# Loading the convolution's tap weights on ScalarE's DMA queue and converting them first, in a fused attention and gated FFN kernel

## Chip, cores and metric

One core of one Trainium2 chip. The metric is the device time of one execution in microseconds (us), median over runs; lower is better.

## What is computed

Inputs are float32 in kind, but the weights `w_in`, `conv_w` and `w_out` come as 64-bit floats, viewed as pairs of 32-bit words.

```python
# 4 batches, 8 heads, 768 positions, head width 64; chunks of 32 queries
for c in range(nc):                       # a window of 16 + 32 + 8 keys and 8 memory keys
    scores = scale * q_c @ k_full.T
    a = softmax(scores)
    out[:, :, c_start:c_end] = a @ v_full
x = out as (batch, 768, 512)
h = np.maximum(x @ w_in, 0.0)             # 512 -> 1024
conv_out = sum(conv_w[k] * hp[:, k:k + S] for k in range(3))   # 3 taps for each of 1024 channels
gate = 1.0 / (1.0 + np.exp(-conv_out))
return h * gate @ w_out                   # 1024 -> 512
```

## The kernel before

The work is cut into 32 attention pieces (batch, half of the sequence, pair of heads), 32 blocks of hidden channels (batch, 128 channels), and the output products. Matmul operands are kept as two parts, high and low, so that three matmuls make one product. `from_f64` makes the two parts from the two 32-bit words of each weight: it loads a tile `w` (pool `w64`, 4 buffers), makes a working copy `w_top` (2 buffers) with an absolute value on ScalarE (L306), and then goes through integer and float steps on VectorE, GpSimd and ScalarE. It is called once for the tap weights (128x24, kind `s`), 8 times for `w_in` and 8 times for `w_out` (128x512 each). The last step for the taps adds the two parts into `cw` (L815), from which the gating of every block of channels takes its three taps (L598 and L602 for the middle one, L607 for the outer ones).

Each engine runs its instructions in the order in which they are written, and that order is fixed by hand: the functions first register 1818 operations in a list (`plan.op`), numbered as they are registered, and `Plan.run` then issues them in the sequence of the table `ORDER`. Operations 0 to 10 are the tap weights: 0 the load, 1 the absolute value, 2 a maximum on GpSimd (L310), 3 to 6 four steps on VectorE (L316, L323, L342, L371), 7 an add on GpSimd (L377), 8 the high part on ScalarE (L379), 9 the low part on GpSimd (L382), 10 the sum `cw` on VectorE (L815). Operations 570 on are `w_in`. All loads of the kernel are issued by SyncE (SP), in the order of the same table. Buffers of a pool are handed out first in, first out, when an operation first needs one.

Ahead of the plan ScalarE makes `minus`, a negated identity (L283), with the load of its function table before it, and GpSimd clears some buffers.

The first operations of `ORDER` before are

```python
ORDER = [
    570, 571, 572, 573, 580, 574, 581, 582, 0, 583, 586, 12, 575, 11, 577, 587, 584, 588, 29, 585, 28, 45, 14, 15,
```

with operations 1 to 10 spread over the following lines.

Of the kernel before, what the change touches and what calls it, by code (L numbers as in the profile page):

```python
# [11 lines left out]
U32 = mybir.dt.uint32  # L12
# [199 lines left out]
RATE = 405  # L212
# [11 lines left out]
def attention_then_gated_ffn(  # L224
# [10 lines left out]
    nc = tc.nc  # L235
# [14 lines left out]
    plan = Plan()  # L250
# [36 lines left out]
    def load(dst, src, w):  # L287
        size = 1
        for x in src.shape:
            size *= x  # L290
        plan.op("DMA", size * 4 / RATE, lambda: nc.sync.dma_start(out=dst(), in_=src), w=w)

    def from_f64(src, hi, lo, key, n, kind):
        w = Tile("w64")
# [646 lines left out]
```

## Time and profile before

| | |
|---|---|
| time, median of 3 runs | 337.82 us (336.71 to 338.04) |
| the profiled execution's own time | 337.24 us |
| its span, first to last instruction | 335.5 us |
| TensorE busy (PE) | 322.1 us, 96% of the span |
| VectorE busy (DVE) | 296.4 us, 88% |
| ScalarE busy (ACT) | 222.6 us, 66% |
| GpSimd busy (POOL) | 51.2 us, 15% |
| granted TensorE clock | 0.998 of full |
| moved by DMA | 60.87 MB, all of the kernel's own on one queue, q1 |

PE counts matmuls, PEld the loads of their stationary operand, SPq the DMA issues of SyncE. A time on the timeline is counted from the start of the span. The execution's own time is 1.7 us longer than its span.

### The profile page before, as it was taken

The page shows a single profiled execution, that of the slowest core. Times are in us where ns is not written, and L with a number is a line of the kernel's source. Part 1 is how long each engine was busy: PE and PEld are TensorE (multiplying, and loading weights), DVE is VectorE, ACT ScalarE, POOL GpSimd, SP SyncE. Part 2 cuts the span into 40 slices and gives each one's busy share as a digit, 9 for nine tenths or more (in the row PEclk, how much of TensorE's full clock was granted, in tenths as well). Part 3 has the DMA queues.
Part 4 walks back from the last instruction along what each step waited for, and adds up shares of the span by engine and source line. Part 5 has one row for each costly group of instructions (what it writes and reads, how often), then busy time and mean ns, then how long its engine had stood idle before and what let it go on. Part 6 is the DMA issues. An engine that isn't in the chain of part 4 may idle for free.

```text
span 335.5 us, 8308 instructions
## 1 busy us (share of the span) xinstructions
PE 322.1 (96%) x3259; PEld 305.1 (91%) x3259; DVE 296.4 (88%) x516; ACT 222.6 (66%) x502; POOL 51.2 (15%) x72
## 2 busy tenths in 40 slices
PE   0899999999999999999999999999999999999995
PEld 0689999999999999899988878999999999999995
DVE  3998998999999989899999999999999999599311
ACT  3588896887787879759787527658886486355210
POOL 2150310302104010410020312000000600700000
PEclk9999999999999999999999999999999999999999
DMA  8999998699697969650412545131032642011013
GB/s 278 401 372 345 388 342 291 218 300 293 202 328 230 295 193 342 218 167 34 129 61 80 195 134 198 75 146 47 2 109 64 195 135 96 26 56 63 33 65 110
DMA packets 31144, 60.87 MB, mean 181 GB/s; under 512 B 3584, under 2 KB 18048, under 8 KB 31104
## 3 DMA queue, kind: packets, MB, share of 16 engines
q1 hardware_dynamic: 31104, 60.33, 53.3%
q8 instruction: 26, 0.43, 0.5%
q14 instruction: 14, 0.11, 0.1%
HBM read 47.93 MB, written 12.39 MB: 180 GB/s over the span
## 4 chain that ended last, share of the span: by engine, by line
PE 89%; DMA 5%; DVE 2%; ACT 2%; issue 1%; SPq 0%; ACTq 0%
PE f L577 38%; PE f L736 15%; PE f L793 10%; PE s L736 7%; PE ta L540 7%; PE s L427 6%; PE ta L736 4%; DMA w<-in_w_out_dram 2%; PE ta L491 2%; DMA out_dram<-k 1%; DMA w<-in_w_in_dram 1%; ACT e L462 1%; ACT w_top L306 0%; PE f L355 0%; DVE w_top L323 0%
## 5 line engine op out<-in xcount | busy, mean ns | idle before, releaser
L577 PE MATMUL f<-u,w_in_hi 128*128 128x384 f32 x512 | 140.8, 343 | 0.6 <-ACT u L587 0.6
L577 PEld LDWEIGHTS f<-u,w_in_hi 128*128 128x128 f32 x512 | 93.2, 188 | 2.7 <-ACT u L587 1.1
L577 PE MATMUL f<-u,w_in_lo 128*128 128x384 f32 x256 | 86.0, 336 | 0.0
L607 DVE SCALAR_TENSOR_TENSOR u<-u,cw,u 128x767 f32<-128x767 f32 x64 | 64.4, 1027 | 0.1
L577 PEld LDWEIGHTS f<-u,w_in_lo 128*128 128x128 f32 x256 | 48.2, 188 | 0.2
L644 DVE TENSOR_TENSOR u<-u,u 128x768 fp32r<-128x768 f32 (+1 forms) x55 | 46.5, 871 | 0.8 <-ACT u L641 0.8
L641 ACT CAST u<-u 128x768 fp32r<-128x768 f32 (+1 forms) x56 | 41.1, 765 | 8.3 <-PE s L736 2.8
L736 PE MATMUL f<-w_in_hi,u 128*128 128x256 f32 x216 | 45.0, 282 | 0.0
L587 ACT ACTIVATE u<-f 128x384 f32<-128x384 f32 x64 | 30.6, 490 | 15.9 <-PE f L577 15.0
L736 PEld LDWEIGHTS f<-w_in_hi,u 128*128 128x128 f32 x216 | 36.0, 188 | 0.0
L616 DVE SCALAR_TENSOR_TENSOR u<-u,u 128x768 f32<-128x768 f32 x32 | 31.4, 993 | 0.4 <-ACT u L611 0.4
L793 PE MATMUL f<-w_out_hi,u 128*128 128x512 f32 x96 | 31.6, 397 | 0.0
L462 ACT ACTIVATE e<-s,top 128x64 f32<-128x64 f32 x132 | 29.3, 324 | 3.4 <-DVE w L509 1.6
L611 ACT ACTIVATE u<-u 128x768 f32<-128x768 f32 x32 | 26.8, 847 | 6.1 <-DVE u L607 6.0
L736 PE MATMUL f<-w_in_lo,u 128*128 128x256 f32 x108 | 30.3, 281 | 0.0
L598 ACT ACTIVATE u<-u,cw 128x768 f32<-128x768 f32 x30 | 28.3, 944 | 2.7 <-DVE z L476 1.3
L479 POOL TENSOR_TENSOR e<-e,z 128x384 f32<-128x384 f32 x22 | 20.6, 936 | 54.1 <-DVE z L476 35.3
L753 ACT COPY w<-f 128x256 f32<-128x256 f32 x18 | 6.6, 374 | 27.3 <-PE f L736 22.8
L427 PE MATMUL s<-k,u 128*64 128x64 f32 x672 | 24.7, 224 | 0.0
L427 PEld LDWEIGHTS s<-k,u 128*64 128x64 f32 x672 | 21.8, 138 | 3.1 <-issue 2.2
L759 DVE TENSOR_TENSOR k<-s,w 128x256 f32<-128x256 f32 x18 | 7.6, 422 | 17.1 <-PE s L736 9.6
L651 POOL TENSOR_TENSOR u<-u,u 128x384 f32<-128x384 f32 x9 | 10.8, 1200 | 74.6 <-DVE u L616 62.0
(99 smaller groups left out, 609.6 us busy)
## 6 DMA issues: line engine op xcount, KB each, us to landing
u<-in_q_dram SPq DMA_DIRECT2D x32, 384.0 KB, 6.2
u<-in_v_dram SPq DMA_DIRECT2D x25, 384.0 KB, 5.4
k<-in_k_dram SPq DMA_DIRECT2D x28, 252.0 KB, 4.9
out_dram<-k SPq DMA_DIRECT2D x36, 128.0 KB, 1.7
w<-in_w_in_dram SPq DMA_DIRECT2D x8, 512.0 KB, 6.7
w<-in_w_out_dram SPq DMA_DIRECT2D x8, 512.0 KB, 5.9
y_dram<-u SPq DMA_DIRECT2D x8, 384.0 KB, 2.8
u<-y_dram SPq DMA_DIRECT2D x8, 384.0 KB, 3.4
```

What stands on the lines that cost most here:

```text
L427: nc.tensor.matmul(s.t[j * D : (j + 1) * D, o : o + KW], lhsT=q_[:, c], rhs=k_t.t[:, c * STEP : c * STEP + KW], start=True, stop=True,)
L462: A.activation(keys(e)[:, g // 2, g % 2], s_()[:, g // 2, g % 2], AF.Exp, bias=top.t[:, g : g + 1], scale=SCALE)
L577: nc.tensor.matmul(f.t[:, :TW], lhsT=w_in_p[c][:, part, col : col + P], rhs=x.t[:, a * TW : (a + 1) * TW], start=(cc == 0 and i == 0), sto ...
L587: "A", act(TW, True), lambda: A.activation(h.t[:, hf * TW : (hf + 1) * TW], f.t[:, :TW], AF.Relu, scale=0.5), (f,), ((h, hf),)
L598: plan.op("A", act(S, ptr=1), lambda: A.activation(c.t, h.t, AF.Copy, scale=w[1]), H, (c,))
L607: lambda j=j, to=to, at=at: V.scalar_tensor_tensor(out=c.t[:, to], in0=h.t[:, at], scalar=w[j], in1=c.t[:, to], op0=ALU.mult, op1=ALU.add) ...
L611: plan.op("A", act(S), lambda: A.activation(c.t, c.t, AF.Tanh), (c,), (c,), table="exp")
L616: lambda: V.scalar_tensor_tensor(out=y.t, in0=c.t, scalar=1.0, in1=h.t, op0=ALU.add, op1=ALU.mult),
L641: plan.op("A", act(n), lambda: A.copy(out=hi(), in_=src()), (y,), (k_hi,))
L644: lambda: (V if eng == "V" else G).tensor_tensor(out=low(), in0=src(), in1=hi().bitcast(F32), op=ALU.subtract),
L736: nc.tensor.matmul(ps.t[:, :n], lhsT=l[a](), rhs=w[c], start=(first and j == 0 and m == 0), stop=(j == hf - 1 and m == 2), skip_group_chec ...
L793: nc.tensor.matmul(ps.t[:, :n], lhsT=gs[b, fc][a].t[:, tt * P : (tt + 1) * P], rhs=w_out_p[c][:, fc, o : o + n], start=(fc == 0 and i == 0 ...
```

## The change

The tap weights' load is issued from ScalarE's queue and not from SyncE's, and operations 0 to 10 stand first in `ORDER`. All other operations keep their order among themselves.

```diff
 ORDER = [
-    570, 571, 572, 573, 580, 574, 581, 582, 0, 583, 586, 12, 575, 11, 577, 587, 584, 588, 29, 585, 28, 45, 14, 15,
+    0, 1, 2, 3, 4, 5, 6, 7, 8, 9, 10, 570, 571, 572, 573, 580, 574, 581, 582, 583, 586, 12, 575, 11, 577, 587, 584,
...
-    def load(dst, src, w):
+    def load(dst, src, w, queue=nc.sync):
         size = 1
         for x in src.shape:
             size *= x
-        plan.op("DMA", size * 4 / RATE, lambda: nc.sync.dma_start(out=dst(), in_=src), w=w)
+        plan.op("DMA", size * 4 / RATE, lambda: queue.dma_start(out=dst(), in_=src), w=w)
...
-        load(lambda: w.t[:, :n].rearrange("p n w -> p (n w)"), src.bitcast(U32), (w,))
+        load(lambda: w.t[:, :n].rearrange("p n w -> p (n w)"), src.bitcast(U32), (w,), nc.scalar if key == "cw2" else nc.sync)
```

On ScalarE, at the start of the program, the difference reads as follows (`w_89` to `w_92` are the four buffers of pool `w64`, `w_top_93` and `w_top_94` the two of the working copy, `cw_hi` the taps' high part; lines with - stood there before, lines with + now).

```order
 L283 ACT_TABLE_LOAD
 L283 ACTIVATE w_out_hi<-ident 128x128
-L306 ACTIVATE w_top_93<-w_89 128x512
+L291 DMA w_89<-in_conv_w_dram 128x48
+L306 ACTIVATE w_top_93<-w_89 128x24
+L379 CAST cw_hi<-w_top_93 128x24
 L306 ACTIVATE w_top_94<-w_90 128x512
```

The load's issue, the taps' absolute value and their high part have moved in front of the first absolute value of `w_in`, and behind the table load and `minus`.

VectorE began before with the first block of `w_in`:

```order
L936 UNCONDITIONAL_BRANCH
L310 TENSOR_SCALAR w_top_93<-w_top_93 128x512
L316 TENSOR_SCALAR w_top_93<-w_top_93 128x512
L323 SCALAR_TENSOR_TENSOR w_top_93<-w_89,w_top_93 128x512
L310 TENSOR_SCALAR w_top_94<-w_top_94 128x512
```

and begins now with the taps:

```order
L936 UNCONDITIONAL_BRANCH
L316 TENSOR_SCALAR w_top_93<-w_top_93 128x24
L323 SCALAR_TENSOR_TENSOR w_top_93<-w_89,w_top_93 128x24
L342 TENSOR_SCALAR w_89<-w_top_93 128x24
L371 SCALAR_TENSOR_TENSOR w_89<-w_89 128x24
L815 TENSOR_TENSOR cw<-cw_hi,cw_lo 128x24
L310 TENSOR_SCALAR w_top_94<-w_top_94 128x512
L316 TENSOR_SCALAR w_top_94<-w_top_94 128x512
```

All five of the taps' steps on VectorE now stand ahead of the 11 steps of `w_in` and of the first maximum over scores (L436), which followed those 11 before and follows them now.

## Rows read from the trace of the kernel before

**Rows 1.** Chain of waits, first 26 us: start us, us, what.
```profile
4.43 0.67 ACT w_top L306
...
5.12 0.44 DVE w_top L310
...
5.58 0.44 DVE w_top L316
...
10.60 0.48 DVE top L436
...
13.82 1.55 PE s L427 x24
...
19.30 0.85 PE s L427 x24
```
**Rows 2.** All waits of TensorE: waited for, us in total, times, longest us.
```profile
PE s L427 <- DMA u<-in_q_dram: 7.7, 1, 7.7
PE s L427 <- DVE e L441: 0.9, 1, 0.9
PE f L577 <- ACT u L587: 0.6, 1, 0.6
PE s L427 <- ACT e L462: 0.6, 1, 0.6
```
**Rows 3.** ScalarE's timeline from the start: start us, us, instruction, [idle before].
```profile
0.72 1.28 ACT L283 ACT_TABLE_LOAD   x1 [0.72 <-PEq L928]
2.02 0.31 ACT L283 ACTIVATE w_out_hi<-ident 128x128 fp32r<-128x128 f32 x1
```
**Rows 4.** SyncE's timeline: the issue of the tap weights' load.
```profile
1.64 0.42 SPq L291 DMA_DIRECT2D w<-in_conv_w_dram  x1
```
**Rows 5.** DMA issues of the whole run: count, KB each, median us to landing.
```profile
out_dram<-k SPq DMA_DIRECT2D x36, 128.0 KB, 1.7
...
w<-in_conv_w_dram SPq DMA_DIRECT2D x1, 24.0 KB, 4.2
```
**Rows 6.** DMA issues in the first microsecond.
```profile
w<-in_w_in_dram SPq DMA_DIRECT2D x1, 512.0 KB, 3.7
```
**Rows 7.** Busy time by stretch; the last two columns are DMA share and GB/s.
```profile
2.70:4.40 1.70, 0.00 (x0) 0.00 (x0) 0.00 (x0) 0.00 (x0) 0.16 (x6) 1.00 0.97 378
```
**Rows 8.** Groups by line and shape, the taps' ten instructions: busy us, mean ns | idle.
```profile
L310 POOL TENSOR_SCALAR w_top<-w_top 128x24 f32<-128x24 f32 x1 | 0.4, 430 | 0.0
L371 DVE SCALAR_TENSOR_TENSOR w<-w 128x24 f32<-128x24 uint32 x1 | 0.4, 367 | 0.0
...
L382 POOL TENSOR_TENSOR cw_lo<-w_top,cw_hi 128x24 f32<-128x24 f32 x1 | 0.2, 240 | 0.0
L377 POOL TENSOR_TENSOR w_top<-w_top,w 128x24 f32<-128x24 f32 x1 | 0.2, 235 | 0.1
L306 ACT ACTIVATE w_top<-w 128x24 f32<-128x24 f32 x1 | 0.2, 217 | 0.0
...
L379 ACT CAST cw_hi<-w_top 128x24 fp32r<-128x24 f32 x1 | 0.2, 195 | 0.0
L342 DVE TENSOR_SCALAR w<-w_top 128x24 uint32<-128x24 uint32 x1 | 0.2, 178 | 0.0
L815 DVE TENSOR_TENSOR cw<-cw_hi,cw_lo 128x24 f32<-128x24 f32 x1 | 0.2, 175 | 0.0
L316 DVE TENSOR_SCALAR w_top<-w_top 128x24 uint32<-128x24 uint32 x1 | 0.2, 170 | 0.0
L323 DVE SCALAR_TENSOR_TENSOR w_top<-w,w_top 128x24 uint32<-128x24 uint32 x1 | 0.1, 146 | 0.0
```
**Rows 9.** VectorE's timeline, where the taps are finished.
```profile
41.04 0.17 DVE L815 TENSOR_TENSOR cw<-cw_hi,cw_lo 128x24 f32<-128x24 f32 x1
```
**Rows 10.** ScalarE's timeline, first reader of the taps.
```profile
55.06 0.93 ACT L598 ACTIVATE u<-u,cw 128x768 f32<-128x768 f32 x1
```
**Rows 11.** Waits of SyncE's queue, 14 to 60 us: the one on a `w64` buffer.
```profile
SPq L291 <- DVE w_in_lo L394: 4.4, 1, 4.4
```

178 rows, old and new, of the table ORDER are left out of this document.

## Prediction

> **What bounds the kernel now.** I read the waits of TensorE first, because the profile has it busy for 96% of the span. It waits four times in all [rows 2]: 7.7 us for the first queries, 0.9 us and 0.6 us among the first four groups of scores, and 0.6 us once in the FFN's matmuls (L577), later on. So from 13.82 us, where the fourth group of scores starts, to its last matmul TensorE has one gap of 0.6 us; whatever moves its work at 13.82 us moves the end by as much. Next I ask what sets 13.82 us, in the chain of waits [rows 1]. It is neither the queries nor the scores. The first block of `w_in` lands, ScalarE takes its absolute value at 4.43 us, VectorE starts on it at 5.12 us, and VectorE then has no pause until it reaches the first maximum over scores at 10.60 us; from there the chain goes through the first softmax steps to TensorE at 13.82 us. The start of the kernel is a VectorE chain that begins when ScalarE reads `w_in`.
>
> The third view is who needs the taps. Their sum is ready at 41.04 us [rows 9] and first read at 55.06 us [rows 10]: 14 us of slack. Having them earlier is worth nothing by itself.
>
> **The change, step by step.**
>
> *The load's issue.* On SyncE one issue of 0.42 us goes [rows 4], and the loads of keys and queries behind it start that much sooner. The first scores can then start some 0.4 us earlier, but VectorE gets to them only at 10.60 us, so I cost this at nothing; VectorE's steps on `w_in` hide it. On ScalarE the issue stands behind the table load and `minus`, which ScalarE runs from 2.02 us for 0.31 us [rows 3]. It can begin when `minus` starts (2.02) or when it ends (2.33); I take 2.33. That is later than the 1.64 us of before.
>
> *The landing.* No load was issued by ScalarE before, so I bound it. The shortest time from issue to landing in the trace is 1.7 us, a 128 KB store; the longest that fits is 4.2 us, that of this load itself [rows 5], which was queued behind 1 MB of `w_in`. In between stands the first load of all: 3.7 us with nothing ahead of it [rows 6], of which its 512 KB take 1.35 us at the 378 GB/s of that stretch [rows 7]; the other 2.3 us are the fixed part of a load at this point of the program. For 24 KB I take 2.3 us and 0.3 us for sharing busy DMA engines, 2.6 us, near the row with nothing ahead because the new queue is empty. Landing at 2.33 + 2.6 = 4.93 us; bounds 2.02 + 1.7 = 3.72 and 2.33 + 4.2 = 6.53.
>
> The Trainium skill bears on the choice. The row shows 4.2 us behind other loads in one queue [rows 5]; the page "DMA: Bandwidth & Descriptors", section "Queues, rings and completion order", says that each DMA engine takes turns between the queues that have work, a packet at a time. By that rule the taps do not wait for the whole backlog of SyncE's queue and the cost below stays near 2.5 us; if the engines served the oldest request first, it would be 4.2 us. No run shows yet which holds here.
>
> *The taps' conversion at the front.* It hops between engines: L306 on ScalarE, L310 on GpSimd, L316, L323, L342, L371 on VectorE, L377 on GpSimd, L379 on ScalarE. With the durations of the taps' own rows [rows 8] this is 0.217 + 0.430 + 0.170 + 0.146 + 0.178 + 0.367 + 0.235 + 0.195 = 1.94 us, and seven hand-overs of about 0.03 us (in [rows 1] a step ends at 4.43 + 0.67 = 5.10 us and the next starts at 5.12) make 2.15 us. Two of these durations look stretched by neighbours: with 0.235 for L310 and 0.178 for L371, as their sister rows have, it is 1.76 us. I take 2.0. Before, these eight stood apart, in other work's shade; now they stand in a row.
>
> *Who stands behind them.* ScalarE runs L306 and L379 of the taps ahead of its first read of `w_in`. That read came at 4.43 us; it now comes at 4.93 + 0.03 + 2.0 = 6.96 us, **2.53 us later**. `w_in` has long landed by then, so nothing is gained back there. The last two steps, L382 and L815 (0.240 + 0.175 us, [rows 8]), run beside the 0.67 us absolute value of `w_in` and cost nothing; without that cover they would cost 0.4 us. VectorE starts on `w_in` 2.53 us later, and the whole chain of [rows 1] behind it moves by that: third and fourth scores, then TensorE's unbroken stretch. By the bounds the shift is 3.72 + 0.03 + 1.76 - 4.43 = 1.08 us at least and 6.53 + 0.03 + 2.15 - 4.43 = 4.28 us at most.
>
> *What is taken out of the middle.* VectorE loses five short steps ahead of 41 us, ScalarE two, GpSimd three, some 1.0, 0.4 and 0.9 us by [rows 8]. The taps held one of four `w64` buffers and one of two working copies; now these go back early, and the 4.4 us for which SyncE waited on a `w64` buffer [rows 11] should go, since that load now gets the buffer that `w_in`'s first block leaves at L349, and no longer the one that is read last at L394. I cost all this at nothing: it is hidden by TensorE, which waits only once after 13.82 us. At best it closes that gap of 0.6 us [rows 2].
>
> **Sum.** 337.24 us of the profiled execution (335.5 of span and 1.7 around it) + 2.5 us = 339.7 us. The profiled execution lies 0.6 us under the median of the three runs; the mean of all four is 337.45, so I forecast from 337.5: **340.0 us**, 0.7% slower. Less than 0.5%, or 1.7 us, can't be told from no change.
>
> **The rivals.**
>
> *The taps arrive early enough (not slower).* Place: ScalarE's first read of `w_in`. If the load lands by 4.0 us, the shift is 4.0 + 2.03 - 4.43 = 1.6 us and the result counts as no change; at the lowest bounds it is 1.1 us, 338.6, and with the late gap closed 338.0. For it: the 1.7 us row and an empty queue. Against it: those 1.7 us belong to stores late in the run, and the loads of the first microseconds need 2.3 us before their bytes are counted. Chance 0.18.
>
> *The taps queue behind `w_in` all the same.* The load takes its old 4.2 us from the new issue, landing at 6.53; shift 4.1 to 4.3 us, 341.7. For it: the DMA engines are fully busy when the load arrives (share 0.97 [rows 7]), and this load's own row. Against it: that row had 1 MB in the same queue. Chance 0.15.
>
> *TensorE stays slow for longer.* The group of 24 scores at 13.82 us takes 1.55 us, the one at 19.30 us 0.85 us [rows 1], though the granted clock reads 1.00 (the level of 2.4 GHz) in both stretches; before the first of these TensorE had paused 0.9 and 0.6 us [rows 2]. With VectorE late, the pause between the second and third groups grows from 0.9 to some 3.5 us, and the fast pace may come a group later: 0.7 us more, 340.7. Against it: the work from 13.82 us on is the same unbroken sequence. Chance 0.12. The Trainium skill, "TensorE: Matmul & The Clock Gate", Part 1, has the clock throttled by default and released by activity, which the slow first groups agree with; the granted clock of the rows does not show it.
>
> *The relief pays (faster).* The start costs little and freed buffers let everything run ahead. It needs the read of `w_in` to stay at 4.43 us, so taps landed by 2.4 us, before any DMA has brought 1 MB, and even then only the 0.6 us gap is there to win: 336.9, no measurable gain. Only an effect outside these rows gets past 1.7 us. Chance 0.05.
>
> The forecast itself, 339.2 to 341.2 by the landing alone, has 0.50.
>
> **How the numbers follow.** Slower by over 0.5%: the forecast, the queueing case and the slow TensorE, 0.50 + 0.15 + 0.12 = 0.77. Within 0.5%: 0.18. Faster: 0.05. The range leaves out most of the faster case and the extremes of the bounds: 338.5 takes in the upper part of the early-landing case, 341.9 the queueing case.
>
> **What would show it.** In the changed profile: a DMA issue on ScalarE's queue at 2.0 to 2.4 us; the taps' L306 at about 5 us, as ScalarE's next work; ScalarE's first read of `w_in` at about 7.0 us; VectorE's first maximum over scores at about 13.1 us; TensorE's fourth group of scores at about 16.3 us, and from there the old sequence, 2.5 us late to the end; SyncE's 4.4 us wait gone without effect. The forecast is wrong if ScalarE reads `w_in` before 6.1 us, if TensorE's shift at the fourth scores is 2.5 us but shrinks further on (then slack was hidden in TensorE's busy time), or if TensorE's pace changes.

## The result, and the profile after

The changed kernel takes 340.84 us (median of 5 runs, 340.56 to 341.52); the kernel before, with two more runs, 337.06 us (335.71 to 338.04). The ratio is 1.0117, 95% interval 1.0091 to 1.0144: **slower by 3.8 us**, where 2.5 us were forecast. It lies in the range, and its sign and its place are as forecast; its parts are not. The profiled execution took 341.52 us, the longest of the five; its span is 339.4 us against 335.5, so 3.9 us are to be found in the traces.

ScalarE's timeline of the changed kernel, which answers to [rows 3] and to the first of [rows 1]:

```profile
0.72 1.28 ACT L283 ACT_TABLE_LOAD   x1 [0.72 <-PEq L928]
1.34 0.38 ACTq L291 DMA_DIRECT2D w<-in_conv_w_dram  x1
...
5.77 0.22 ACT L306 ACTIVATE w_top<-w 128x24 f32<-128x24 f32 x1 [3.44 <-DMA w<-in_conv_w_dram]
...
7.63 0.21 ACT L379 CAST cw_hi<-w_top 128x24 fp32r<-128x24 f32 x1 [1.64 <-POOL w_top L377]
...
7.75 1.25 ACT L306 ACTIVATE w_top<-w 128x512 f32<-128x512 f32 x2
```

Two things are to be seen. The issue (ACTq is ScalarE's queue of DMA issues) starts at 1.34 us, while the table load is still running and before `minus`, which starts at 2.02. And the load still lands only at 5.74 us, 4.4 us later. ScalarE then waits for the whole conversion and first reads `w_in` at 7.75 us, where it did so at 4.43: 3.32 us late.

DMA of the changed kernel from 4.4 to 6 us, by queue (packets, MB, share of the 16 engines), and below it the issue of the taps with its time to landing:

```profile
q1 hardware_dynamic: 240, 0.55, 90.1%
q10 hardware_dynamic: 144, 0.02, 8.1%
```
```profile
w<-in_conv_w_dram ACTq DMA_DIRECT2D x1, 24.0 KB, 4.4
```

q10 is the new queue, and 144 is the number of its packets in the whole run: not one of them moved before 4.4 us, three microseconds after the issue.

The chain of waits of the changed kernel from VectorE's first step on `w_in` (start us, us, what):

```profile
8.45 0.44 DVE w_top L310
...
13.93 0.48 DVE top L436
...
17.14 1.55 PE s L427 x24
18.69 0.83 PE ta L491 x3
19.53 1.71 PE f L355 x2
21.23 0.85 PE f L357 x2
22.09 1.38 PE ta L540 x24
23.47 0.48 PE ta L491 x3
```

and the same stretch of TensorE in the kernel before, of which [rows 1] showed only the first line:

```profile
13.82 1.55 PE s L427 x24
15.36 0.83 PE ta L491 x3
16.20 1.32 PE f L355 x2
17.52 0.45 PE f L357 x2
17.97 0.85 PE ta L540 x24
18.82 0.48 PE ta L491 x3
```

VectorE starts 3.33 us late (5.12 to 8.45), and so do the first maximum (10.60 to 13.93) and the fourth scores (13.82 to 17.14). Then TensorE loses more: L355 takes 1.71 us and not 1.32, L357 0.85 and not 0.45, L540 1.38 and not 0.85. At the second transposes (L491 at 23.47) it is 4.65 us late. Whether that belongs to the change or to this execution, the traces of the experiments tell.

The waits of TensorE, beside [rows 2]:

```profile
PE s L427 <- DMA u<-in_q_dram: 7.8, 1, 7.8
PE s L427 <- DVE e L441: 4.1, 1, 4.1
...
PE f L577 <- ACT u L587: 0.4, 1, 0.4
```

The wait on VectorE's L441 grew from 0.9 to 4.1 us. The late one on L587 shrank from 0.63 to 0.44.

To see what becomes of the delay I took, in each trace, the start of the same group of transposes by the identity, and subtracted the kernel before:

| start in the kernel before, us | the change, us late |
|---|---|
| 15.29 | 3.33 |
| 18.75 | 4.65 |
| 64.75 | 4.50 |
| 129.3 | 4.63 |
| 142.53 | 4.46 |
| 197.58 | 4.46 |

So nothing happens to it in 180 us of TensorE's work but some 0.2 us at the gap at 140 us. The last 0.56 us go in the tail: the last copy from PSUM waited 1.24 us for an earlier store in the kernel before and only for its matmuls in the changed one.

```profile
332.46 0.37 ACT L753 COPY k<-f 128x256 f32<-128x256 f32 x1 [1.24 <-DMA out_dram<-k]
```
```profile
336.38 0.37 ACT L753 COPY k<-f 128x256 f32<-128x256 f32 x1 [0.69 <-PE f L736]
```

The sum of the profiled executions is then 3.33 (late start) + 1.32 (slow TensorE) - 0.19 (to 4.46, mostly the gap at 140 us) - 0.56 (tail) = 3.9 us.

SyncE's wait of 4.4 us on L394 [rows 11] is gone from the changed trace; TensorE's waits above show no gain from it.

### The profile page after: what moved, and what is told of

Read it like the earlier page. It is cut to its first block, busy times and chain, and to the rows that moved or that the text cites. A ratio compares the mean times of both kernels' runs of the same rounds, so it can differ in the third digit from the quotient of the medians.

```text
span 339.4 us, 8310 instructions
## 1 busy us (share of the span) xinstructions
PE 323.4 (95%) x3259; PEld 305.9 (90%) x3259; DVE 296.7 (87%) x516; ACT 222.3 (65%) x502; POOL 51.1 (15%) x72
## 4 chain that ended last, share of the span: by engine, by line
PE 89%; DVE 6%; ACT 2%; issue 1%; POOL 1%; POOLq 0%; DVEq 0%
PE f L577 37%; PE f L736 15%; PE f L793 10%; PE s L736 8%; PE ta L540 6%; PE s L427 6%; PE ta L736 4%; PE ta L491 2%; DVE u L607 1%; ACT e L462 1%; DVE w_top L323 1%; PE f L355 1%; DVE top L436 0%; DVE w_top L316 0%; POOL a_d L261 0%
## 5 line engine op out<-in xcount | busy, mean ns | idle before, releaser
L587 ACT ACTIVATE u<-f 128x384 f32<-128x384 f32 x64 | 30.5, 490 | 16.0 <-PE f L577 15.1
L546 ACT CAST u<-ta 128x384 fp32r<-128x384 f32 x32 | 15.3, 480 | 11.6 <-PE ta L540 11.5
```

The costliest lines, as they stand in the source:

```text
L587: "A", act(TW, True), lambda: A.activation(h.t[:, hf * TW : (hf + 1) * TW], f.t[:, :TW], AF.Relu, scale=0.5), (f,), ((h, hf),)
```

## Experiments

Theories to tell apart: the loss is the wait for the taps' landing, or it is the conversion's length; the landing is late because of ScalarE's queue, or because of what was issued ahead on the other one; and TensorE's 1.3 us come from its pauses, or from waits, or from this one execution.

### The load back on SyncE's queue

```diff
-    0, 1, 2, 3, 4, 5, 6, 7, 8, 9, 10, 570, 571, 572, 573, 580, 574, ...
+    570, 580, 0, 1, 2, 3, 4, 5, 6, 7, 8, 9, 10, 571, 572, 573, 574, ...
-        load(..., (w,), nc.scalar if key == "cw2" else nc.sync)
+        load(..., (w,))
```

> The taps converted first, as in the change, but their load back on SyncE's queue, third behind the two w_in loads, where it stood before. Theory A (the position of the conversion costs, and ScalarE's queue gained nothing): the taps land at 5.8 us, ScalarE reads w_in at 7.8 us, TensorE's fourth scores start at 17.2 us; time 340.8 us, within 0.7 of the change. Theory B (ScalarE's queue makes the load late, since it was issued at 1.34 us and took 4.4 us): the taps land by 4.5 us, time 339.5 us or less.

340.29 us (6 runs; kernel before beside it 336.95), ratio 1.0100, 1.0077 to 1.0123. Its ScalarE:

```profile
6.00 0.22 ACT L303 ACTIVATE w_top<-w 128x24 f32<-128x24 f32 x1 [3.67 <-DMA w<-in_conv_w_dram]
...
7.98 1.24 ACT L303 ACTIVATE w_top<-w 128x512 f32<-128x512 f32 x2
```

Theory A. Issued at 1.65 us behind both `w_in` loads in one queue it lands at 5.97 us; on its own queue, issued 0.3 us sooner, it landed 0.2 us sooner. The second queue gave nothing but the earlier issue, and not always that: in the three other traces below that issue this load from ScalarE at 1.34 us behind both `w_in` loads it took 4.7 to 4.8 us, so that it landed at 6.0 to 6.1.

TensorE in this trace, with a pause as long as the change's (4.06 us there) and no loss of pace behind it:

```profile
15.27 1.55 PE L424 MATMUL s<-u,u 128*64 128x64 f32 x24 [4.22 <-DVE e L438]
17.37 1.55 PE L424 MATMUL s<-u,u 128*64 128x64 f32 x24 [0.55 <-ACT e L459]
...
22.18 0.55 PE L488 MATMUL ta<-ident,e 128*128 128x128 f32 x3
```

From the fourth scores to the second transposes it takes 4.81 us; the kernel before took 4.93, the change 6.26.

### The load on SyncE's queue, ahead of `w_in`

```diff
-        load(..., (w,), nc.scalar if key == "cw2" else nc.sync)
+        load(..., (w,))
```

> The taps converted first, their load on SyncE's queue ahead of both w_in loads. Theory A (the wait for the taps' landing sets the loss): with nothing ahead they land at 3.0 to 3.4 us, the conversion's 2.0 us ends at 5.3, ScalarE reads w_in 0.9 us later than in the kernel before, in place of 3.3; time 338.0 to 339.0 us. Rival (the loss is the conversion's length and the loads' order hardly matters): 340.5 us or more.

337.68 us (12 runs, 335.89 to 340.14), ratio 1.0018, 0.9997 to 1.0039.

```profile
2.37 0.22 ACT L306 ACTIVATE w_top<-w 128x24 f32<-128x24 f32 x1
4.37 0.21 ACT L379 CAST cw_hi<-w_top 128x24 fp32r<-128x24 f32 x1 [1.77 <-POOL w_top L377]
4.90 0.66 ACT L306 ACTIVATE w_top<-w 128x512 f32<-128x512 f32 x1 [0.32 <-DMA w<-in_w_in_dram]
```
```profile
w<-in_conv_w_dram SPq DMA_DIRECT2D x1, 24.0 KB, 1.6
```

The same conversion at the same place, and most of the loss is gone. With nothing ahead the taps land 1.6 us after their issue, sooner than expected, and the conversion ends at 4.58 us, before `w_in` lands. What is left, 0.47 us (4.90 against 4.43), is `w_in` itself, issued one issue later. So **the landing decides whether the conversion costs anything**: there is room for 2 us of it before `w_in` arrives, if the taps are there by 2.4 us. In the change they were ready at 5.77 us, 1.34 us after the old read of `w_in`, and the 1.98 us of conversion came on top.

The profiled execution is the slowest of the twelve (340.14 us). TensorE in it has the old short pause before the third scores (0.80 us), and from the fourth scores to the second transposes it takes 6.28 us, as long as in the change:

```profile
14.28 1.55 PE L427 MATMUL s<-u,u 128*64 128x64 f32 x24 [0.55 <-ACT e L462]
...
20.56 0.55 PE L491 MATMUL ta<-ident,e 128*128 128x128 f32 x3
```

### ScalarE's issue first of all

```diff
-    A.activation(minus, ident, AF.Copy, scale=-1.0)
...
-        plan.op("DMA", ..., lambda: queue.dma_start(out=dst(), in_=src), w=w)
+        plan.op("DMA", ..., lambda: (queue.dma_start(out=dst(), in_=src), queue is nc.scalar and A.activation(minus, ident, AF.Copy, scale=-1.0)), w=w)
```

> As the change, with the taps' load issued from ScalarE ahead of its table load and of minus, so at about 0.75 us in place of 1.34. Theory A (the DMA engines serve the two queues in the order of issue): it now stands behind one w_in load only and lands at about 4.4 us; ScalarE reads w_in at 6.4 us; time 339.3 us. Rival B (the queues take turns): it lands at about 3.2 us, time 338.3 us. Rival C (a load from ScalarE's queue lands behind all of w_in whenever it is issued): 5.7 us, time 340.8 us.

339.91 us (6 runs), ratio 1.0085, 1.0059 to 1.0111.

```profile
0.73 0.40 ACTq L290 DMA_DIRECT2D w<-in_conv_w_dram  x1
...
4.57 0.22 ACT L305 ACTIVATE w_top<-w 128x24 f32<-128x24 f32 x1 [1.80 <-DMA w<-in_conv_w_dram]
...
6.54 1.22 ACT L305 ACTIVATE w_top<-w 128x512 f32<-128x512 f32 x2
```

The times are theory A's to within 0.2 us: landing at 4.54 us, read of `w_in` at 6.54. Its mechanism is not shown by them, for the packets moved in turns here. DMA from 2 to 4.2 us, by queue:

```profile
q1 hardware_dynamic: 183, 0.68, 80.1%
q10 hardware_dynamic: 144, 0.02, 8.3%
```

All 144 packets of the taps moved in that stretch, none before it, and about one for one with those of q1: from 2.5 to 3 us 40 beside 38. That is rival B's taking of turns, and it did not bring the load forward, for with each of its small packets about one of q1's large ones moved. My 3.2 us for that rival left this out, so this run does not tell A from B. The changed kernel does: its 144 packets stood still until 4.4 us, while q1 moved 224.

The placements together: nothing ahead, landed 1.6 us after the issue; one `w_in` load issued at the same moment on the other queue, 3.8; two issued ahead, 4.4 to 4.8 (other queue, four traces) and 4.2 to 4.3 (same queue, three traces). The time is somewhat above the expected 339.3; the 2.1 us of late read do not make all of the 3.0 us between the medians, though they lie within the interval.

### TensorE kept busy, first attempt

```diff
+    def idle_work(count):
+        for _ in range(count):
+            nc.tensor.matmul(plan.pools["f"][3][:, :P], lhsT=ident, rhs=ident, start=True, stop=True)
+
+    idle_work(20)
...
+            if n == 1:
+                idle_work(15)
```

The second addition stands in `scores`, after the second group. Each added matmul stands as two in the trace.

> The change, with 20 matmuls of the identity on TensorE from 1.4 us on and 15 more between the second and third groups of scores, into a PSUM buffer that is overwritten later. Theory (TensorE's idle start and the 4.1 us pause keep it slow until 23 us): the groups of 24 scores take 0.85 us at 17 us, the stretch from the fourth scores to the second transposes takes some 4 us and not 6.3; time 338.5 to 339.6 us. Rival (the pace there has another cause, such as waits for operands): no change, 340.8 us, or slower by what the added matmuls hold up.

341.53 us (6 runs, 339.19 to 341.92), ratio 1.0123, 1.0092 to 1.0154: no gain in the median. Its profile tells why. TensorE's timeline (idle before in brackets) and its granted clock by stretch (the fourth number, after busy time and count):

```profile
10.29 3.62 PE L287 MATMUL f<-ident 128*128 128x128 f32 x30
15.30 0.92 PE L433 MATMUL s<-u,u 128*64 128x64 f32 x24 [1.40 <-DVE e L449]
17.40 1.55 PE L433 MATMUL s<-u,u 128*64 128x64 f32 x24 [1.18 <-ACT e L470]
```
```profile
16.00:16.50 0.50, 0.22 (x8) 1.00 1.04 390
16.50:17.00 0.50, 0.00 (x0) 0.72 1.05 386
17.00:17.50 0.50, 0.10 (x2) 0.50 1.08 397
...
23.00:24.00 1.00, 1.00 (x19) 0.73 1.05 414
24.00:25.00 1.00, 1.00 (x27) 1.00 0.53 192
```

The 24 matmuls of the third scores take 0.92 us, and after pauses of 1.40 and 1.18 us the same 24 take 1.55 us: the granted clock has gone from 1.00 (2.4 GHz) to 0.50 (1.2 GHz), and comes back between 23 and 24 us, after six microseconds of unbroken work. The kernels without added matmuls show 1.55 us for these groups and a granted clock of 1.00. So at the start of a trace, before its first recorded change, the column does not show the level; the duration of an equal group does. (The first clock record that the traces hold, of full clock, begins at 17.0 us in the kernel before and at 23.2 in the change.) I had left two pauses open, and TensorE fell back in them.

### TensorE kept busy in all three pauses

```diff
+    idle_work(16)
...
+            idle_work({1: 18, 2: 4}.get(n, 0))
```

> The change with added matmuls of the identity in all three pauses of TensorE ahead of the fourth scores: 16 at the start, 18 after the second scores, 4 after the third. Theory (TensorE's pauses cost the change its fast pace until 23 us): the granted clock stays at 1.00, the fourth scores take 0.85 us, and the second transposes start at about 21.2 us, where the change had 23.5; time 338.2 to 339.2 us. What is left over the kernel before is then the late read of w_in less what TensorE gains against the slow groups of that kernel too. Rival (pace is not what the change lost): 340.5 us or more.

339.17 us (7 runs, 338.31 to 341.16), ratio 1.0084, 1.0054 to 1.0114; the change stood at 1.0117.

```profile
16.25 1.16 PE L287 MATMUL f<-ident 128*128 128x128 f32 x8
17.50 0.92 PE L433 MATMUL s<-u,u 128*64 128x64 f32 x24
...
21.15 0.55 PE L498 MATMUL ta<-ident,e 128*128 128x128 f32 x3
```

The fourth scores take 0.92 us, and the second transposes come at 21.15 us, 2.4 us late against the kernel before and not 4.65, although ScalarE read `w_in` even later (8.10 us). Against the kernel before, run beside each, the median is 2.5 us late and the change's 3.8; the intervals overlap, and the profiled execution, the slowest of the seven, gave its gain away again later: in the manner of the table above it is 2.4 us late up to 89 us, 3.3 at 117 and 4.46 at 142. That a fast start shortens the stretch from the fourth scores to the second transposes is shown in the trace, 3.65 us where the kernel before took 4.93 and the change 6.26; that it shortens the whole is not clear of noise.

### The load alone

```diff
-    0, 1, 2, 3, 4, 5, 6, 7, 8, 9, 10, 570, 571, 572, 573, ...
+    0, 570, 571, 572, 573, 580, 574, 581, 582, 583, 586, 12, ...
```

Operations 1 to 10 are back at their old places.

> The taps' load on ScalarE's queue as in the change, the conversion back at its old places. Theory (only the conversion's place costs; its rows up to 41 us and SyncE's issue were hidden): the taps land at 5.7 to 6.0 us as in the change, ScalarE reads w_in at 4.4 us, fourth scores at 13.8 us; 337.0 us, within 0.6 of the kernel before. Rival (the second queue disturbs the first loads): w_in lands late and the time is 338.5 us or more.

336.90 us (12 runs, 335.42 to 338.13; the kernel before beside it 336.67), ratio 1.0008, 0.9988 to 1.0029.

```profile
4.54 0.66 ACT L303 ACTIVATE w_top<-w 128x512 f32<-128x512 f32 x1 [2.22 <-DMA w<-in_w_in_dram]
```
```profile
13.93 1.55 PE L424 MATMUL s<-u,u 128*64 128x64 f32 x24 [0.56 <-ACT e L459]
...
20.07 0.55 PE L488 MATMUL ta<-ident,e 128*128 128x128 f32 x3
```

The queue by itself costs and gains nothing that these runs can tell; the loss is the conversion's place, with the landing that it waits for. This profile also warns of reading one trace: its fourth scores start 0.11 us late, its second transposes 1.32 us, for TensorE stayed slow until about 20 us here, with the same pauses as the kernel before. The six traces without added matmuls, side by side (us; the last column is the median over that of the kernel before, run beside it):

| kernel | `w_in` read late | pause before the third scores | fourth scores to second transposes | time over before |
|---|---|---|---|---|
| before | 0 | 0.85 | 4.93 | 0 |
| the load alone | 0.11 | 0.83 | 6.14 | 0.2 |
| SyncE, ahead of `w_in` | 0.47 | 0.80 | 6.28 | 0.7 |
| ScalarE, first of all | 2.11 | 3.10 | 5.67 | 3.0 |
| the change | 3.32 | 4.06 | 6.26 | 3.8 |
| SyncE, third | 3.55 | 4.22 | 4.81 | 3.3 |

The time follows the late read to within 0.9 us. How long the slow pace lasts does not follow the pause: it differs by over a microsecond between traces with a short pause, and as much between traces with a long one. The 1.32 us of the change's trace are therefore not shown to be the change's.

### The kernel before with TensorE kept busy

```diff
+    idle_work(16)
...
+            idle_work({1: 6, 2: 4}.get(n, 0))
```

> The kernel before with the same kind of added matmuls: 16 at the start, 6 after the second scores, 4 after the third. Theory: the fourth scores start at 13.8 us at the fast pace, the work up to the second transposes at 18.8 us shrinks by up to 1.4 us, of which waits on ScalarE's copies give some back; time 335.6 to 336.6 us, less spread between runs, faster than both kernels. Rival (other engines bound that stretch): 337.0 us.

337.39 us (12 runs), ratio 1.0018, 0.9991 to 1.0045: nothing gained, and the theory's 335.6 to 336.6 us missed. In its trace the fast scores win a microsecond, and the next step waits for a load of values:

```profile
14.11 0.92 PE L433 MATMUL s<-u,u 128*64 128x64 f32 x24
...
18.04 0.92 PE L547 MATMUL ta<-a_d,u 128*64 128x64 f32 x24 [1.21 <-DMA u<-in_v_dram]
```

In this execution that load took 9.2 us from issue to landing (7.5 in the kernel before, issued half a microsecond sooner). Whether it is always so late, or was only in this one, stays open. No version beats the kernel before.

## Why the prediction was right or wrong

**The bound: right.** TensorE's unbroken stretch from the fourth scores on carries the delay nearly unchanged in the change's trace (4.65 us at 19 us, 4.46 at 198), and the delay comes through ScalarE's first read of `w_in`, as read from [rows 1] and [rows 2].

**The issue: wrong, and outside its bounds.** I had ScalarE issue the load behind `minus`, at 2.02 to 2.33 us, from the order of its instructions. It came at 1.34 us, during the table load. So ScalarE's DMA issue did not wait here for the arithmetic ahead of it in its order.

**The landing: the step that failed.** I took 2.6 us from issue to landing, 2.3 fixed and 0.3 for sharing busy DMA engines, because the queue was new and empty. It took 4.4 us, just over my upper bound of 4.2, and every packet of it moved after 4.4 us on the timeline. The term that I had at 0.3 us is what failed: with nothing ahead a load took 1.6 us (the load placed ahead of `w_in`), so being behind `w_in` cost 2.8. The rival with 0.15, that the taps queue behind `w_in` all the same, is what happened; its 341.7 us was too high only because the issue was earlier. The two errors partly cancel: landing at 5.74 us against 4.93. That is luck: with the issue at 1.34 us and the rest as I had it, the shift would have been 1.34 + 2.6 + 0.03 + 2.0 - 4.43 = 1.54 us, under the 1.7 us that I said can't be told from no change.

The rule of the Trainium skill that I weighed, in "DMA: Bandwidth & Descriptors", section "Queues, rings and completion order", is that the DMA engines take turns between queues a packet at a time. The trace of ScalarE's issue first of all agrees (144 packets among 183 from 2 to 4.2 us); the changed kernel's does not, where the taps moved nothing until 4.4 us, as if the loads were served in the order of issue. The measurement decides. And where there were turns, they did not give the 2.6 us that I hung on them: the load took 3.8. Nothing here shows how the engines do it, nor whether a longer backlog would be passed.

**The conversion: right.** 2.0 us were forecast from L306 to the end of L379; the trace has 5.77 to 7.75, 1.98 us, and L382 and L815 ran beside the absolute value of `w_in`.

**What was freed: right.** SyncE's issue, its 4.4 us wait, the buffers and the ten instructions taken out of the middle were costed at nothing. With the issue alone gone from SyncE the time is the same (the load alone, 1.0008); with the ten instructions gone from the middle and little paid in front it is not below the kernel before either (the load ahead of `w_in`, 1.0018).

**TensorE's pace: not shown to be the change's.** I gave 0.12 to a slow pace for one group longer after a longer pause, 0.7 us. In the profiled execution it cost 1.32 us. But two kernels with the old short pause lost as much (6.14 and 6.28 us), and the one with the longest pause lost nothing (4.81), so by these traces it is luck of the execution. The page "TensorE: Matmul & The Clock Gate" of the Trainium skill, Part 1, says that pauses bring the clock down to half and activity releases it; the trace with added matmuls agrees in the direction, with 1.00 to 0.50 after pauses of 1.40 and 1.18 us. The late read explains 3.3 of the 3.8 us between the medians; the rest is within the interval, and its cause stays open.

## What to carry to other kernels

Work that nobody needs soon is not free at the front of an engine's order: everything behind it inherits its input's landing, here 3.3 us for 24 KB that were not read until 55 us. Here a second DMA queue did not carry a small load past 1 MB issued earlier (4.4 to 4.8 us, against 4.2 to 4.3 in the same queue); what did was to issue it first, and what it then delays has a price too (0.47 us of `w_in`). Before a slower stretch in one trace is put down to a change, look for the same stretch in other traces: here it took 4.8 to 6.3 us, with the longest time behind the shortest pause.

## What was not expected of the hardware

- ScalarE's queue issued a DMA at 1.34 us, during a table load that ran from 0.72 to 2.00 us and ahead of an activation that precedes it in program order and ran at 2.02.
- A load of 24 KB landed 1.6 us after its issue with nothing ahead, 3.8 us with 0.5 MB issued at the same moment on the other queue, whose packets it moved in turns with, and 4.4 to 4.8 us behind 1 MB issued earlier there, where none of its packets moved for three microseconds.
- TensorE's granted clock reads 1.00 in a trace until its first recorded change, also where equal groups of matmuls take 1.55 us, as they do at 0.50, and not 0.92.
- Gaps far from the change vary between the traces: the one at 140 us was 0.63 us in the kernel before and 0.44 in the changed one, and between 129 and 143 us the delay moved by up to 1.1 us elsewhere (3.3 to 4.46 in the kernel with three fills).
